# Sliding-window attention and a Silu expert layer on one core: attention per head pair in full-array matmuls, row loads cast on chip, an order laid by hand

## Chip, cores and metric

The kernel runs on one core of one Trainium2 chip. The metric is the device time of one execution in microseconds, the median over several runs. Engines are named as the profile names them: PE is TensorE's matmuls, PEld its weight loads, DVE is VectorE, ACT is ScalarE, POOL is GpSimd, SP is SyncE (here it only issues DMAs).

## What is computed

```python
# q, k, v: (8, 8, 576, 64) fp32: batch, head, position, width
scores = (1 / sqrt(64)) * (q @ k.transpose(0, 1, 3, 2))
rel = pos[:, None] - pos[None, :]
scores = where((rel >= 0) & (rel < 64), scores, -1e9)     # a causal window of 64
attn = exp(scores - scores.max(-1)); attn /= attn.sum(-1) + 1e-9
x = (attn @ v).transpose(0, 2, 1, 3).reshape(4608, 512)   # tokens x (heads, width)
h = x @ w_in                                              # 512 -> 2048
out = (h / (1 + exp(-h))) @ w_out                         # 2048 -> 512, fp32
```

## The kernel before

The sequence of 576 positions is cut into nine blocks of 64 queries. Since the window is 64, a block of queries needs 128 keys, its own 64 and the 64 before. Attention works on a pair of heads at a time (`emit_pair_attention`, line 179), 32 pairs in all.

- Loads. For each pair POOL issues two loads of q and two of k (line 187), which are cast from fp32 to bf16 on the way, and six loads of v (lines 199 to 207). v is loaded twice, once in chunks of 128 positions from 0 (`v_even`) and once shifted by 64 (`v_odd`), so that any window of 128 keys starts at partition 0. A 65th column of ones in each head gives the sum of the exponents. All weights are loaded and cast by the same POOL queue: w_in behind the third pair's loads (line 307), w_out behind the seventh's (line 309).
- Transposes. Six matmuls each bring q and k to width-major form (line 222); DVE copies q out of PSUM (line 231), ACT copies k (line 233).
- For each of the two heads: nine score matmuls that use one half of the array's rows (line 244), one exponent over 576 columns on ACT (line 253), one product with a 0/1 mask on DVE (line 255), nine value matmuls of 65 columns (line 263), one reciprocal and one product by it on DVE (lines 273 and 274).
- Nine transposes (line 281) and one copy on DVE (line 289) write the pair's outputs into `bridge`, the bf16 input of the expert layer, four tiles of 128 features by 4608 tokens.

The expert layer works on nine tiles of 512 tokens. The first GEMM of a tile is 16 x 4 matmuls of 512 columns, two output blocks at a time (`emit_moe1_pair`, line 124), each block followed by a Silu on ACT (line 139). The second is 4 x 16 matmuls (line 160), each 16 followed by a DVE copy out of PSUM (line 168) and a store that SP issues (line 170). The first GEMM of a tile is emitted when all pairs of the batches that it covers are emitted (line 314); second GEMMs wait in a list, one block of 128 tokens per pair (line 310). The first eight pairs are those of batches 0 and 1, in turns (line 295). The framework's scheduler orders each engine's instructions from this, by readiness and priority.

PSUM has three buffers for attention, transposes and second GEMMs together (`attn_ps`, line 79) and two for the first GEMM (line 82).

Of the kernel before, what the change touches and what calls it, by code (L numbers as in the profile page):

```python
# [9 lines left out]

MOE_ACT = mybir.ActivationFunctionType.Silu

MOE_UNITS_PER_PAIR = 5


def _build_block_mask(nc, mask, first):
    nc.gpsimd.memset(mask, 1.0)
    nc.gpsimd.affine_select(
        out=mask, in_=mask, compare_op=mybir.AluOpType.is_ge, fill=0.0,  # L20
        base=-1, channel_multiplier=1, pattern=[[-1, 64]],
    )
    nc.gpsimd.affine_select(
        out=mask, in_=mask, compare_op=mybir.AluOpType.is_ge, fill=0.0,
        base=64, channel_multiplier=-1, pattern=[[1, 64]],
    )
    if first:
        nc.gpsimd.affine_select(
            out=mask, in_=mask, compare_op=mybir.AluOpType.is_ge, fill=0.0,
            base=-64, channel_multiplier=1, pattern=[[0, 64]],  # L30
        )
# [3 lines left out]
def kernel(
    ctx: ExitStack,
    tc: tile.TileContext,
    q: bass.AP,
    k: bass.AP,
    v: bass.AP,  # L40
    moe_w_in: bass.AP,
    moe_w_out: bass.AP,
    out: bass.AP,
):
# [3 lines left out]
    d_model, d_ff = moe_w_in.shape
    n_tokens = B * S
    W = 64  # L50
    NBLK = S // W
    NCH = (S + 127) // 128
# [1 line left out]
    NFT = d_ff // 128
    NDC = d_model // 128
    TT = 512
    NTT = n_tokens // TT

    assert S == 576 and D == 64 and d_model == 512 and d_ff == 2048

    PVW = 65
    PVO = 57

    def pv_off(t):
        return PVO + PVW * t

    const_pool = ctx.enter_context(tc.tile_pool(name="const", bufs=1))
    wpool = ctx.enter_context(tc.tile_pool(name="wpool", bufs=1))
    bridge_pool = ctx.enter_context(tc.tile_pool(name="bridge", bufs=1))
    qk_pool = ctx.enter_context(tc.tile_pool(name="qk", bufs=4))  # L70
    qt_pool = ctx.enter_context(tc.tile_pool(name="qt", bufs=2))
    v_pool = ctx.enter_context(tc.tile_pool(name="v", bufs=4))
    e_pool = ctx.enter_context(tc.tile_pool(name="e", bufs=4))
    os_pool = ctx.enter_context(tc.tile_pool(name="os", bufs=4))
    rc_pool = ctx.enter_context(tc.tile_pool(name="rc", bufs=3))
    g_pool = ctx.enter_context(tc.tile_pool(name="g", bufs=18))
# [2 lines left out]
    attn_ps = ctx.enter_context(tc.tile_pool(name="attn_ps", bufs=3, space=bass.MemoryType.PSUM))
    tr_ps = attn_ps  # L80
    moe2_ps = attn_ps
    moe1_ps = ctx.enter_context(tc.tile_pool(name="moe1_ps", bufs=2, space=bass.MemoryType.PSUM))

    identb = const_pool.tile([128, 128], BF16)
    mask_blk = const_pool.tile([128, W], BF16)
    mask_head = const_pool.tile([128, S], BF16)

    def emit_consts():
        nc.gpsimd.memset(identb, 0.0)
# [261 lines left out]
```

## Time and profile before

| what | value |
|---|---|
| median of three runs | 424.79 us (424.58 to 426.48) |
| span of the profiled execution, first to last instruction | 422.7 us |
| PE busy | 351.0 us |
| POOL busy | 251.9 us |
| ACT busy | 174.6 us |
| DVE busy | 139.0 us |
| DMA packets | 157155, 32.49 MB |

The page gives the profiled execution's span, not a time of its own; the times of the runs are some 2 us longer than the span. Busy time of PE counts each matmul to its modelled end, so matmuls that follow each other closely overlap in it, and the distance between two starts is what one of them costs in a row of them. An "idle before" column says how long an engine stood before an instruction, and what ended that.

### The profile page before, as it was taken

To read this page: it belongs to the slowest core of one execution; us is meant where nothing else is said; L and a number is where in the kernel's file an instruction comes from. 1 tells how busy PE (TensorE), PEld (TensorE's weight loads), DVE (VectorE), ACT (ScalarE), POOL (GpSimd) and SP (SyncE) were. 2 spreads that over 40 slices of the span, in tenths; PEclk is the share of its full clock that TensorE was granted. 3 is DMA by queue.
4 is the path that set the end of the run, shared out by engine and by line. 5 is a ranking of instruction groups with operands and counts; after the bars stand their busy time and mean duration, and the time that the engine had idled before them with its cause. 6 is when DMAs were issued, how large, how long until landed. Compare 5 with 4: busy or idle time off the path is not lost.

```text
span 422.7 us, 7509 instructions
## 1 busy us (share of the span) xinstructions
PE 351.0 (83%) x2929; PEld 183.9 (44%) x2976; DVE 139.0 (33%) x292; ACT 174.6 (41%) x270; POOL 251.9 (60%) x493
## 2 busy tenths in 40 slices
PE   0452564799899989998999889988998999999996
PEld 0340453344444544454444544454444444444442
DVE  0350363032631463146314631463135215201011
ACT  1310223394256525651565166516552452342420
POOL 8995998999999798279827892789240000000000
PEclk9999999999999999999999999999999999999999
DMA  8999999999999999599958995899641011001011
GB/s 54 61 103 183 76 86 130 147 87 100 109 102 107 88 88 100 54 79 87 100 56 78 87 99 58 74 87 102 59 53 51 6 46 50 26 0 51 26 51 74
DMA packets 157155, 32.49 MB, mean 77 GB/s; under 512 B 149440, under 2 KB 151488, under 8 KB 157120
## 3 DMA queue, kind: packets, MB, share of 16 engines
q0 software_dynamic: 151936, 22.57, 75.1%
q1 hardware_dynamic: 5184, 9.44, 6.0%
q8 instruction: 24, 0.39, 0.4%
q14 instruction: 11, 0.09, 0.1%
HBM read 45.09 MB, written 9.44 MB: 129 GB/s over the span
## 4 chain that ended last, share of the span: by engine, by line
PE 57%; ACT 15%; POOL 11%; issue 8%; DMA 6%; DVE 2%; another core or an unknown queue 1%; ACTq 0%; POOLq 0%
PE ps L160 22%; PE psa L130 12%; PE psb L130 11%; PE sc_ps L263 5%; ACT e_t L253 5%; ACT gt L139 4%; ACT kt L233 3%; DMA q_nat<-in_q_dram 3%; ACT L253 3%; PE pst L222 3%; POOL q_nat L187 2%; POOL v_odd L207 2%; POOL k_nat L187 2%; PE sc_ps L281 2%; PE sc_ps L244 2%
## 5 line engine op out<-in xcount | busy, mean ns | idle before, releaser
L160 PE MATMUL ps<-w_out_sb,gt 128*128 128x512 bf16 x548 | 142.6, 381 | 2.2 <-issue 1.1
L130 PE MATMUL psa<-bridge,w_in_sb 128*128 128x512 bf16 x276 | 93.2, 383 | 7.8 <-ACT gt L139 4.2
L130 PE MATMUL psb<-bridge,w_in_sb 128*128 128x512 bf16 x281 | 94.0, 382 | 2.3 <-DMA w_in_sb<-in_moe_w_in_dram 1.8
L130 PEld LDWEIGHTS <-w_in_sb 128*128 128x128 bf16 x576 | 55.9, 98 | 76.0 <-issue 17.9
L139 ACT ACTIVATE gt<-psa 128x512 bf16<-128x512 f32 x72 | 43.0, 597 | 89.4 <-PE psa L130 76.0
L160 PEld LDWEIGHTS <-gt 128*128 128x128 bf16 x576 | 51.4, 98 | 54.8 <-ACT gt L139 0.3
L233 ACT COPY kt<-pst 128x576 bf16<-128x576 bf16 x32 | 20.5, 640 | 127.7 <-PE pst L222 123.2
L255 DVE TENSOR_TENSOR e_t<-e_t,mask_head 128x576 bf16<-128x576 bf16 x64 | 29.3, 458 | 109.7 <-ACT e_t L253 107.1
L187 POOL DMA_DIRECT2D q_nat<-in_q_dram x64 | 50.6, 846 | 21.9 <-PE pst L222 18.8
L207 POOL DMA_DIRECT2D v_odd<-in_v_dram x64 | 56.7, 885 | 0.8 <-DMA w_in_sb<-in_moe_w_in_dram 0.8
L199 POOL DMA_DIRECT2D v_even<-in_v_dram x64 | 55.2, 863 | 1.6 <-DMA q_nat<-in_q_dram 0.7
L168 DVE COPY ot<-ps 128x512 f32<-128x512 f32 x36 | 24.9, 691 | 94.1 <-PE ps L160 94.1
L187 POOL DMA_DIRECT2D k_nat<-in_k_dram x64 | 50.6, 841 | 4.5 <-PE pst L222 2.6
L274 DVE TENSOR_TENSOR o_sb<-sc_ps,rcol 64x576 bf16<-64x576 f32 x64 | 47.8, 747 | 1.9
L253 ACT ACTIVATE e_t<-sc_ps 128x576 bf16<-128x576 f32 x64 | 38.2, 648 | 13.7 <-PE sc_ps L244 13.5
L139 ACT ACTIVATE gt<-psb 128x512 bf16<-128x512 f32 x72 | 42.6, 592 | 0.0
L203 POOL DMA_DIRECT2D v_odd<-in_v_dram x64 | 41.7, 651 | 0.4 <-DMA w_in_sb<-in_moe_w_in_dram 0.4
L263 PE MATMUL sc_ps<-v_odd,e_t 128*64 128x65 bf16 x320 | 32.5, 210 | 8.7 <-ACT e_t L253 6.5
L263 PEld LDWEIGHTS <-e_t 128*64 128x64 bf16 x576 | 25.8, 120 | 27.4 <-DVE e_t L255 21.2
L222 PE MATMUL pst<-identb,q_nat 96*128 96x96 bf16 x192 | 16.9, 221 | 22.7 <-DMA q_nat<-in_q_dram 13.2
L244 PE MATMUL sc_ps<-qt,kt 64*128 64x64 bf16 x576 | 21.2, 200 | 16.0 <-ACT kt L233 15.1
L244 PEld LDWEIGHTS <-kt 64*128 64x128 bf16 x576 | 17.7, 100 | 25.5 <-issue 19.3
(32 smaller groups left out, 228.9 us busy)
## 6 DMA issues: line engine op xcount, KB each, us to landing
out_dram<-ot SPq DMA_DIRECT2D x36, 256.0 KB, 2.1
q_nat<-in_q_dram POOLq DMA_DIRECT2D x64, 72.0 KB, 3.1
k_nat<-in_k_dram POOLq DMA_DIRECT2D x64, 72.0 KB, 3.2
v_even<-in_v_dram POOLq DMA_DIRECT2D x64, 64.0 KB, 3.3
v_odd<-in_v_dram POOLq DMA_DIRECT2D x64, 64.0 KB, 3.0
w_in_sb<-in_moe_w_in_dram POOLq DMA_DIRECT2D x8, 256.0 KB, 8.3
w_out_sb<-in_moe_w_out_dram POOLq DMA_DIRECT2D x16, 128.0 KB, 5.0
v_odd<-in_v_dram POOLq DMA_DIRECT2D x64, 8.0 KB, 2.7
```

Source lines behind the costliest of these rows:

```text
L130: nc.tensor.matmul(ps1, lhsT=w_in_sb[:, c, ft * 128:(ft + 1) * 128], rhs=bridge[c][:, t0:t0 + TT], start=(c == 0), stop=(c == NDC - 1),)
L139: nc.scalar.activation(out=gt, in_=ps1, func=MOE_ACT)
L160: nc.tensor.matmul(ps2, lhsT=g_tiles[(j, fc)][:, idx * 128:(idx + 1) * 128], rhs=w_out_sb[:, fc, :], start=(fc == 0), stop=(fc == NFT - 1),)
L187: nc.gpsimd.dma_start(out=nat[:, :, c0:c0 + 64], in_=src[b, h0 + hh, :, :].rearrange("(c p) d -> p c d", p=96),)
L199: nc.gpsimd.dma_start(out=v_even[:, :, c0:c0 + 64], in_=v[b, h0 + hh, 0:512, :].rearrange("(c p) d -> p c d", p=128),)
L203: nc.gpsimd.dma_start(out=v_odd[64:128, 0, c0:c0 + 64], in_=v[b, h0 + hh, 0:64, :],)
L207: nc.gpsimd.dma_start(out=v_odd[:, 1:5, c0:c0 + 64], in_=v[b, h0 + hh, 64:576, :].rearrange("(c p) d -> p c d", p=128),)
L233: nc.scalar.copy(out=dst[:, off:off + S], in_=pst)
L244: nc.tensor.matmul(sc_ps[:, t * W:(t + 1) * W], lhsT=kt[base:base + 64, t * W: t * W + 128], rhs=qt[base:base + 64, t * W:(t + 1) * W], st ...
L253: nc.scalar.activation(out=e_t, in_=sc_ps[:, 0:S], func=mybir.ActivationFunctionType.Exp, scale=scale)
L263: nc.tensor.matmul(sc_ps[0:64, o0:o0 + PVW], lhsT=e_t[:, t * W:(t + 1) * W], rhs=vt[:, chv, hi * 65:(hi + 1) * 65], start=(t == 0 or t == ...
L274: nc.vector.tensor_mul(o_sb[:, :, base:base + 64], pv[:, :, 0:64], rcol[:, :, None].to_broadcast([64, NBLK, W]),)
```

## The change

The kernel is written anew around the same mathematics.

- q and k of a pair are loaded by one DMA each, as fp32 in rows of 512 bytes; SP issues them (POOL for pairs 4 to 7). They are cast to bf16 on chip: in the first batch by DVE (q) and ACT (k), later by POOL.
- v is loaded once, in three DMAs with a cast, and DVE copies it between the two halves of the partitions (`fix_v`).
- The transposed q of a pair is written into a tile `qbd` that holds head 0 in partitions 0 to 63 and head 1 in 64 to 127, each beside zeros. One matmul with all 128 rows of k then gives the scores of both heads for one block of queries, 128 columns; one value matmul with 128 exponent columns gives both heads' outputs, 130 columns, of which each head uses its half.
- A unit of attention is a group: a pair and three blocks of queries (`scores`, `values`, `to_bridge`). There are 96. The outputs are written into one of four zeroed tiles `obd`, and a matmul against two stacked unit matrices adds and transposes them; ACT copies the result to `bridge`.
- The order of the program is kept (`manual_schedule`). Batch 0 is prepared alone. A tile's first GEMM is emitted with the transposes of the next four pairs between its matmuls, one step after every six; its second GEMM with attention steps, one after every three. A step holds the scores of one group, the values of the group two steps back and the bridge matmuls of the group four steps back. Beside the nine second GEMMs stand 12, 8, 12, 12, 8, 12, 12, 8 and 0 groups.
- Tile 0's first GEMM is split into columns 0 to 192 and 192 to 512, and its second GEMM goes over all four token blocks at once, in order of the weights' arrival.
- PSUM is four buffers for both GEMMs and four for attention, used in turn.

```diff
+    ctx.enter_context(tc.manual_schedule())
...
+    moe_ps = ctx.enter_context(tc.tile_pool(name="moe_ps", bufs=4, space=bass.MemoryType.PSUM))
+    at_ps = ctx.enter_context(tc.tile_pool(name="at_ps", bufs=4, space=bass.MemoryType.PSUM))
...
+    def load_qk(u, eng):
+        b, pj = divmod(u, NP)
+        for nm, src in (("q", q), ("k", k)):
+            t = nat_pool.tile([96, 6, 128], FP32, name=f"{nm}_nat", tag=f"{nm}_nat")
+            eng.dma_start(
+                out=t,
+                in_=src[b, 2 * pj:2 * pj + 2].rearrange("h (g p c) d -> p (h g) (c d)", g=3, c=2),
+            )
+            nat[(nm, u)] = t
...
+    def load_w_in():
+        for f in range(8):
+            f0 = f * 256
+            nc.gpsimd.dma_start(
+                out=w_in_sb[:, :, f0:f0 + 256],
+                in_=w_in[:, f0:f0 + 256].rearrange("(c p) f -> p c f", p=128),
+            )
...
+    def cast(u, nm, copy):
+        t = natb_pool.tile([96, 6, 128], BF16, name=f"{nm}_natb", tag=f"{nm}_natb")
+        copy(
+            out=t.rearrange("p m (h d) -> p h m d", h=2),
+            in_=nat.pop((nm, u)).rearrange("p (h g) (c d) -> p h (g c) d", h=2, c=2),
+        )
...
+    def fix_v(u):
+        t = vv[u % NK].rearrange("p t (h x) -> p t h x", h=2)
+        nc.vector.tensor_copy(out=t[0:64, 2:9:2, :, 0:64], in_=t[64:128, 1:9:2, :, 0:64])
+        nc.vector.tensor_copy(out=t[64:128, 0:8:2, :, 0:64], in_=t[0:64, 1:9:2, :, 0:64])
...
+    def scores(u, g):
+        i = u % NK
+        sp = at_ps.tile([128, 3, 2, 64], FP32, name="sp", tag="ap")
+        for x in range(3):
+            t = 3 * g + x
+            nc.tensor.matmul(
+                sp[:, x], lhsT=kt[i][:, t * 64:t * 64 + 128],
+                rhs=qbd[i][:, :, t * 64:(t + 1) * 64],
+                start=(x == 0), stop=(x == 2),
+            )
+        e = e_pool.tile([128, 3, 2, 64], BF16, name="e", tag="e")
+        nc.scalar.activation(out=e, in_=sp, func=ACTF.Exp, scale=scale)
+        nc.vector.tensor_mul(e, e, mask0 if g == 0 else mask)
...
+    def values(u, g):
...
+        pv = at_ps.tile([128, 3, VW], FP32, name="pv", tag="ap")
+        for x in range(3):
+            nc.tensor.matmul(
+                pv[:, x, :], lhsT=e[:, x].rearrange("p h i -> p (h i)"),
+                rhs=vv[i][:, 3 * g + x, :], start=(x == 0), stop=(x == 2),
+            )
...
+        nc.vector.reciprocal(out=rc, in_=pv.rearrange("p x (h y) -> p x h y", h=2)[:, :, :, 64])
+        for hh in range(2):
+            p0 = hh * 64
+            nc.vector.tensor_mul(
+                ob[p0:p0 + 64, :, p0:p0 + 64],
+                pv[p0:p0 + 64, :, hh * 65:hh * 65 + 64],
+                rc[p0:p0 + 64, :, hh:hh + 1].to_broadcast([64, 3, 64]),
+            )
...
+    def to_bridge(u, g):
...
+        op = at_ps.tile([128, 3, 64], FP32, name="op", tag="ap")
+        for x in range(3):
+            nc.tensor.matmul(op[:, x, :], lhsT=ob[:, x, :], rhs=twoi,
+                             start=(x == 0), stop=(x == 2))
...
+        nc.scalar.copy(out=bridge[pj][:, c0:c0 + 192], in_=op.rearrange("p x i -> p (x i)"))
...
+    for u in range(4, 8):
+        load_qk(u, nc.gpsimd)
+    for f in range(4):
+        load_w_out(f)
+    for u in range(4, 8):
+        load_v(u)
+    for f in range(4, 8):
+        load_w_out(f)
...
+    interleave(mm1(0, 0, 192), 7, first, lead=2)
+    for i in range(4, 8):
+        zeros(i)
+    for u in range(4, 8):
+        cast(u, "q", pcopy)
+        cast(u, "k", pcopy)
...
+    for j in range(NTT):
...
+        for u in nxt:
+            load_qk(u, nc.sync)
+        interleave(mm1(j, 192, TT) if j == 0 else mm1(j), 6, ins, lead=30 if j == 0 else 4)
+        interleave(mm2(j, j == 0), 3, attention_steps(part[j]), lead=2)
+        for u in nxt:
+            load_v(u)
+            cast(u, "q", pcopy)
+            cast(u, "k", pcopy)
```

## Rows read from the trace of the kernel before

**Rows 1.** The page, part 1: busy us (share of the span) and instructions of each engine.
```profile
PE 351.0 (83%) x2929; PEld 183.9 (44%) x2976; DVE 139.0 (33%) x292; ACT 174.6 (41%) x270; POOL 251.9 (60%) x493
```

**Rows 2.** Stretches: length, then PE, PEld, DVE, ACT, POOL busy (instructions), clock, DMA.
```profile
0.00:75.00 75.00, 32.55 (x409) 24.39 (x413) 24.98 (x56) 16.46 (x25) 67.17 (x143) 1.00 1.14 101
...
214.79:257.43 42.64, 39.02 (x350) 20.36 (x356) 16.98 (x37) 21.02 (x33) 29.58 (x56) 1.00 0.92 80
361.90:418.70 56.80, 56.01 (x254) 24.55 (x254) 5.99 (x9) 17.36 (x32) 0.00 (x0) 1.00 0.10 38
418.70:422.70 4.00, 0.02 (x1) 0.00 (x0) 0.69 (x1) 0.00 (x0) 0.00 (x0) 1.00 0.17 66
```

**Rows 3.** Timeline of POOL, first 70 us: start, length, what [idle before <-releaser].
```profile
1.38 1.60 POOL L187 DMA_DIRECT2D q_nat<-in_q_dram  x2 [0.86 <-POOLq L335]
...
26.30 4.39 POOL L111 DMA_DIRECT2D w_in_sb<-in_moe_w_in_dram  x8
...
39.92 0.76 POOL L207 DMA_DIRECT2D v_odd<-in_v_dram  x1 [0.78 <-DMA w_in_sb<-in_moe_w_in_dram]
...
43.47 1.49 POOL L187 DMA_DIRECT2D q_nat<-in_q_dram  x2
...
47.33 0.58 POOL L203 DMA_DIRECT2D v_odd<-in_v_dram  x1
...
50.72 1.55 POOL L187 DMA_DIRECT2D q_nat<-in_q_dram  x2
```

**Rows 4.** Timeline of PE, at 73 us and in the period from 214.79.
```profile
73.18 1.44 PE L130 MATMUL psa<-bridge,w_in_sb 128*128 128x512 bf16 x3 [0.69 <-ACT gt L139]
...
219.49 2.76 PE L160 MATMUL ps<-w_out_sb,gt 128*128 128x512 bf16 x12
222.44 0.22 PE L263 MATMUL sc_ps<-v_odd,e_t 128*64 128x65 bf16 x1 [0.19 <-ACT e_t L253]
...
222.72 0.20 PE L263 MATMUL sc_ps<-v_odd,e_t 128*64 128x65 bf16 x1
222.85 0.39 PE L160 MATMUL ps<-w_out_sb,gt 128*128 128x512 bf16 x1
...
225.84 0.43 PE L281 MATMUL sc_ps<-identb,o_sb 64*128 64x64 bf16 x9
...
226.25 0.42 PE L222 MATMUL pst<-identb,k_nat 96*128 96x96 bf16 x6
```

**Rows 5.** Groups by line and shape, whole run: busy us, mean ns | idle before.
```profile
L274 DVE TENSOR_TENSOR o_sb<-sc_ps,rcol 64x576 bf16<-64x576 f32 x64 | 47.8, 747 | 1.9
L139 ACT ACTIVATE gt<-psa 128x512 bf16<-128x512 f32 x72 | 43.0, 597 | 89.4 <-PE psa L130 76.0 <-PE ps L160 7.0 <-remote 6.3
...
L253 ACT ACTIVATE e_t<-sc_ps 128x576 bf16<-128x576 f32 x64 | 38.2, 648 | 13.7 <-PE sc_ps L244 13.5
...
L255 DVE TENSOR_TENSOR e_t<-e_t,mask_head 128x576 bf16<-128x576 bf16 x64 | 29.3, 458 | 109.7 <-ACT e_t L253 107.1
...
L168 DVE COPY ot<-ps 128x512 f32<-128x512 f32 x36 | 24.9, 691 | 94.1 <-PE ps L160 94.1
...
L253 ACT ACT_TABLE_LOAD x14 | 18.0, 1283 | 0.2
...
L273 DVE RECIPROCAL rcol<-sc_ps 64x9 f32<-64x9 f32 x64 | 13.2, 207 | 5.6 <-PE sc_ps L263 5.1
...
L97 POOL COPY mask_head<-mask_blk 128x64 bf16<-128x64 bf16 x8 | 1.5, 280 | 0.0
...
L89 POOL MEMSET identb<- 128x128 bf16 x1 | 0.3, 302 | 0.0
L18 POOL MEMSET mask_head<- 128x64 bf16 x1 | 0.2, 248 | 0.0
```

**Rows 6.** Timeline of ACT and DVE in the period from 214.79: exponents, mask products.
```profile
221.25 1.19 ACT L253 ACTIVATE e_t<-sc_ps 128x576 bf16<-128x576 f32 x2
221.93 1.00 DVE L255 TENSOR_TENSOR e_t<-e_t,mask_head 128x576 bf16<-128x576 bf16 x2 [6.90 <-ACT e_t L253]
```

More of the change, by code (lines that the diff above doesn't have):

```diff
@@ L10 @@
 BF16 = mybir.dt.bfloat16
[L12 to L31, printed above, removed]
@@ L34, with kernel @@
-@with_exitstack
[L35 to L44, printed above, removed]
+ACTF = mybir.ActivationFunctionType
+GE = mybir.AluOpType.is_ge
+@with_exitstack
+def kernel(ctx, tc, q, k, v, w_in, w_out, out):
     nc = tc.nc
     B, H, S, D = q.shape
[L48 to L52, printed above, removed]
-    scale = 1.0 / float(D) ** 0.5
[L54 to L76, printed above, removed]
-    o_pool = ctx.enter_context(tc.tile_pool(name="o", bufs=4))
[L79 to L89, printed above, removed]
@@ new lines, in transposes @@
+    def transposes(u, nm, copies):
+        t = natb.pop((nm, u))
+        pst = at_ps.tile([128, 6, 96], BF16, name="pst", tag="ap")
+        for m in range(6):
+            nc.tensor.matmul(
+                pst[:, m, :], lhsT=t[:, m, :], rhs=ident[0:96, 0:96],
+                is_transpose=True, start=(m == 0), stop=(m == 5),
+            )
+        src = pst.rearrange("x (g c) p -> x g p c", c=2)
+        if nm == "q":
+            d = qbd[u % NK].rearrange("x h (g p c) -> x h g p c", g=3, c=2)
+            copies[0](out=d[0:64, 0], in_=src[0:64])
+            copies[1](out=d[64:128, 1], in_=src[64:128])
+        else:
+            d = kt[u % NK][:, 64:64 + S].rearrange("x (g p c) -> x g p c", g=3, c=2)
+            copies[0](out=d, in_=src)
@@ new lines, in interleave @@
+    def interleave(stream, every, steps, lead=0):
+        steps = iter(steps)
+        for n, _ in enumerate(stream):
+            if n >= lead and (n - lead) % every == 0:
+                st = next(steps, None)
+                if st is not None:
+                    st()
+        for st in steps:
+            st()
+    vcopy, acopy, pcopy = nc.vector.tensor_copy, nc.scalar.copy, nc.gpsimd.tensor_copy
+    groups = {b: [(4 * b + pj, g) for g in range(NG) for pj in range(NP)] for b in range(B)}
@@ new lines @@
+    todo = [gr for b in range(1, B) for gr in groups[b]]
+    beside = [12, 8, 12, 12, 8, 12, 12, 8, 0]
+    part, last = [], []
+    for n in beside:
+        part.append(todo[:n])
+        todo = todo[n:]
+        last.append(max([u for u, _ in part[-1]] + last[-1:]))
+    for u in range(4):
+        load_qk(u, nc.sync)
+    consts()
+    for u in range(4):
+        load_v(u)
+    load_w_in()
+    for i in range(4):
+        zeros(i)
+    nc.vector.tensor_copy(out=twoi[0:64, :], in_=ident[0:64, 0:64])
@@ new lines @@
+    nc.vector.tensor_copy(out=twoi[64:128, :], in_=ident[64:128, 64:128])
+    nc.vector.tensor_copy(out=mask0, in_=mask)
+    nc.vector.memset(mask0[0:64, 0], 0.0)
+    for i in range(NOB):
+        nc.vector.memset(obd[i].bitcast(FP32), 0.0)
+    first = list(attention_steps(groups[0], ahead=2))
+    for u in range(4):
+        cast(u, "q", vcopy)
+        cast(u, "k", acopy)
+        transposes(u, "q", (vcopy, acopy))
+        transposes(u, "k", (acopy,))
+        fix_v(u)
+        if u >= 2:
+            first.pop(0)()
```

342 lines of the change are left out of this document (143 added, 199 removed).

## The prediction, made before the changed kernel ran

> **What bounds the kernel now.** I read the page first, then the stretches by stage, then the queue of each engine inside a stretch. On the page TensorE is busy 351.0 of 422.7 us, GpSimd 251.9 and VectorE 139.0 [rows 1]. The stretches say which of them holds each stage. In the first 75 us GpSimd is busy for 67.17 and TensorE for 32.55; from 129.48 to 300.09 one period of 42.65 us, a batch each, comes four times, with 39.02 us of TensorE and 29.58 of GpSimd in it; and the last 57 us are nearly all expert matmuls [rows 2].
>
> What fills the first 75 us is GpSimd issuing loads. Its timeline starts one pair's loads at 43.47 and the next pair's at 50.72, so 7.25 us a pair whatever TensorE does: four loads of q and k at 0.75 each, v in six pieces, four memsets [rows 3]. Eight pairs are loaded before the first expert tile starts at about 72 us. The weights stand in the same queue: eight loads of w_in issued from 26.30 in 4.39 us, and a load behind them still waits for one of them at 39.92, 13.6 us later [rows 3].
>
> The period I price by the distance between starts, not by the busy column. Twelve matmuls of 512 columns cover 2.76 us with a last one of 0.38, so 0.216 each; six transposes of 96 columns 0.42 with a last of 0.21, so 0.042; nine of 64 columns 0.43, so 0.030; nine of 65 columns from 222.44 to 222.72, so 0.035 [rows 4]. A period is then 128 x 0.216 + 48 x 0.042 + 108 x 0.030 + 72 x 0.035 = 35.4 us, and 7.2 us are waits. That is about what can be gained in each of them; the start holds the rest. At 73.18 three matmuls of 512 columns take 1.44 us, where 0.216 apart they would take 0.81 [rows 4]: that is the lower of TensorE's two clock levels (1.2 and 2.4 GHz), though the clock column of the stretches reads 1.00 there [rows 2]. TensorE had been mostly idle before it.
>
> **The change part by part.** *Full-array attention matmuls.* A pair had 18 score and 18 value matmuls of 64 and 65 columns; it gets 9 and 9 of 128 and 130. The columns that stream through are the same, so at 0.418 ns a column (from 0.042 at 96 and 0.216 at 512) they cost 0.056 each, 1.0 us a pair as against 1.2. By itself this part is worth nearly nothing; the trace has none of 128 columns; the bounds are 0.042 and 0.216, nearest to the lower one. What changes is the evacuation: three groups a pair, each with one exponent, one mask product, one reciprocal and two products.
>
> *The start.* One batch, not two, is prepared, q and k of it on SP's queue. GpSimd's queue up to the second expert GEMM of tile 0 decides, I think. Launch and constants about 3.2 us (the first load now goes at 1.38 [rows 3], and some six constants at about 0.3 [rows 5]); 12 loads of v, per pair two as dear as a load of q and one of the short kind at 0.58 [rows 3], 8.3; 8 of w_in, in more and shorter rows, at 0.75 like q's rows (bounds 0.55, today's, and 0.75), 6. The loads of q and k for pairs 4 to 7 stand behind these and wait for w_in to land, as the load at 39.92 does now: first issue at 11.5 plus 13.6, so 25, and one more issue, 26. Then 4 of w_out at 0.55 (as w_in's now), 12 of v, 4 of w_out: 12.7, so 38.6. Then eight casts of 96x768 float to bf16, which TensorE's transposes for tile 0 wait for. The nearest rows are a 128x64 copy of 0.28 and memsets of 0.248 and 0.302 for 64 and 128 columns [rows 5]: by that slope, 0.84 ns a column, a cast is 0.87 and 0.8 in a stream; by the copy's 4.4 ns a column throughout it is 3.4. I take 0.8, since the slope comes from two rows; the start ends at 38.6 + 6.4 + 1 = 46. VectorE reaches the same point by about 38 (memsets 8, four pairs at 3, the steps of batch 0 at 8 to 16, by the rates below), so it is cover with 8 us to spare, and GpSimd's turn. Below, 40; above, 67.
>
> *After 46 us* TensorE has left: 64 + 8 x 128 expert matmuls at 0.216, 235.0; 84 groups of attention at 3 x (0.056 + 0.056 + 0.030) = 0.425, 35.8; transposes of 24 pairs, 288 x 0.042, 12.1. The 64 extra matmuls of the split tile 0 lie before 46.
>
> *The steps.* Fixed and per-element prices of VectorE and ScalarE come from pairs of rows: 64x576 in 0.747 and 128x512 in 0.691 on VectorE is 1.04 ns an element plus 0.15; the mask product of 576 in 0.458 goes at half that per element; ScalarE's 576 in 0.648 and 512 in 0.595 is 0.83 plus 0.17 [rows 5]. A group's exponent (384) is then 0.49, its mask product 0.36, its reciprocal 0.21 like today's [rows 5], its two products (192 each) 0.35 each. VectorE has 1.26 us in a step for which TensorE has 0.425 + 3 x 0.216 = 1.07. And the four PSUM buffers go round: a full step takes three, so the third matmul group of a step needs the buffer that the step before gave to its values, and that comes free when VectorE has done both products. From the first score matmul: last one ends at 0.33, exponent 0.37 to 0.86, mask to 1.25, reciprocal to 1.43, products to 2.1, seen at 2.16 (hand-overs of about 0.04: the first of the two exponents from 221.25 lasts 0.65, and the mask product starts at 221.93 [rows 5, 6]). The next step's third group then goes at 2.16, and after its 0.09 and three expert matmuls the step after begins: two steps in 2.90, so 1.45 each and a wait of 0.38. Full steps (all three parts present) are 8 of a 12-group part and 4 of an 8-group part: 5 x 8 + 3 x 4 = 52, so 19.8 us. Without the buffer wait it is 0; at one and a half times these VectorE durations two steps take 3.53, a wait of 0.69 each, 36.
>
> *Smaller terms.* The 0.69 us copy of each finished output tile [rows 5] stands in the same VectorE queue; in 13 cases it falls between full steps and moves the mask product by 0.5: 6.5. At each second GEMM the first exponent waits behind the last Silu and a table load of 1.28 [rows 5], about 0.85 beyond TensorE's cover: 8 x 0.85 = 6.8. Going from a short matmul to a 512 one starts 0.13 after the last, not 0.035 [rows 4]: 0.09 on the 44 steps that do not wait anyway, 4. At 46 VectorE is behind with the four pairs' copies (11.6 us of work from 39.5 on), which holds the first values up by 4, and TensorE, idle before, starts its dense work at the lower clock, as at 73.18 [rows 4], where the matmuls stood 0.43 apart; taken for some 4 us, 2: 6. The end is as now, 4.0 from the last matmul on [rows 2].
>
> What I cost at nothing, and its cover: v is shifted by VectorE instead of loaded twice; with the copies of q and k that is 2.9 us a pair (two copies of 576 at 0.75, two of 512 at 0.68), 11.6 a tile under a first GEMM of 15.9, and if that cover fails it is the excess per tile. The casts and 12 loads of v are 15 us of GpSimd a tile of 40. SP's loads of the next four pairs each wait for a cast to free a buffer, and the output stores are queued behind them; the casts are done a GEMM earlier. Silu, 16 x 0.6 [rows 5], and the q copies stay under the first GEMM.
>
> **Sum:** 46 + 235.0 + 35.8 + 12.1 + 19.8 + 6.5 + 6.8 + 4 + 6 + 4.0 = 376.0 us of span. The profiled execution's span is 422.7, the median 424.79, so 2.1 us lie outside: 378 us against 424.79.
>
> No row shows VectorE and GpSimd reading on-chip memory together; GpSimd's only copies now are eight at the start [rows 5]. The Trainium skill, "SBUF — State Buffer" (Who interferes with whom), says that a VectorE instruction with two inputs there and a GpSimd one that reads there lock each other out for a whole instruction. The mask product and the cast are such a pair; by this rule the sum would be about 390, the third rival.
>
> **The rivals.**
> - *No waits in the steps* (341): the buffers or VectorE are quicker than priced and the four smaller waits go too, less 37 of waits. For it: today's period loses only 7.2 us on a longer chain. Against it: 1.26 exceeds 1.07 anyhow.
> - *Dear casts* (400): 3.4 us each moves the start to 67. Per tile GpSimd would have 8 x 3.4 + 8.3 = 35.5 us, just under a tile, so no more than the start is lost. For it: 0.28 for 64 columns. Against it: the two memsets.
> - *Casts and mask products exclude each other* (390): 48 casts of 0.87 stand beside 84 mask products in tiles of 40 us; casts fill a sixth of the time, so 14 meetings at up to 0.87, 12 us. All of them meeting is 42 us, 420.
> - *VectorE becomes the bound* (430, slower): its place is every tile after 46 us. At my durations it has 197 us there (six first GEMMs at 11.6, five second ones at 12 x 1.26 + 4 x 0.69 = 17.9, three with 8 groups at 12.8); the stretches without it, start, last tile, end, add 94. It decides from 1.44 times my durations on (378 = 94 + 1.44 x 197) and makes the kernel slower from 1.7 times on: 94 + 1.7 x 197 = 430. For it: strided two-byte reads and shifts between partition halves have no row. Against it: today's product of 576 and copy of 512 fit one price [rows 5].
>
> **How the numbers follow.** The forecast gets 0.43, no waits 0.24, dear casts 0.13, exclusion 0.08, VectorE 0.12, of which 0.03 within 0.5% of now (2.1 us, about what a measurement of this kernel can tell from no change) and 0.09 above. Faster is 0.88. The range reaches from just under the no-wait case, 338, to just over the dear casts, 404; what is left out is VectorE's 0.12 and the lower third of the no-wait case.
>
> **What would show it.** In the changed profile: first matmul of tile 0's second GEMM near 46 us, with GpSimd full until the casts; full steps 1.4 to 1.5 us apart, the wait before the bridge matmuls ended by VectorE's products; VectorE near 240 us in all; GpSimd well under 200; a tile with twelve groups near 40 us, one with eight near 36. It is wrong if casts last over 2 us, if steps follow each other at 1.1 or at 2 us, or if TensorE waits on transposes in tiles 1 to 6.

## The result, and the profile of the kernel after

The changed kernel takes 396.21 us (median of 4 runs, 395.85 to 396.95) against 424.69: a ratio of 0.932, 95% interval 0.929 to 0.935, so 28.5 us less. The profiled execution's span is 394.6, and 1.6 us lie outside.

The page's part 1, as [rows 1]:

```profile
PE 329.4 (83%) x2423; PEld 180.0 (46%) x2464; DVE 232.9 (59%) x596; ACT 206.3 (52%) x410; POOL 133.4 (34%) x185
```

GpSimd falls from 251.9 to 133.4 us, VectorE rises from 139.0 to 232.9, TensorE loses 21.6. The stretches, cut by this kernel's stages: the start to the second GEMM of tile 0, that GEMM and a whole period from tile 2's second GEMM to tile 3's; columns as in [rows 2]:

```profile
0.00:61.20 61.20, 31.29 (x332) 25.71 (x333) 37.05 (x122) 30.44 (x70) 48.66 (x73) 0.97 1.25 192
61.20:89.25 28.05, 22.82 (x173) 12.40 (x174) 23.37 (x57) 13.85 (x31) 11.76 (x16) 0.94 0.56 54
141.87:183.70 41.83, 36.84 (x280) 19.50 (x284) 27.96 (x68) 23.60 (x46) 15.12 (x20) 1.00 0.55 97
```

The start is 61.2 us long, with TensorE busy for half of it. A period with twelve groups lasts 41.83 us, with 36.84 of TensorE: 5.0 are waits. GpSimd's queue in the start, as [rows 3], then VectorE's in the same time:

```profile
14.18 6.30 POOL L87 DMA_DIRECT2D w_in_sb<-in_moe_w_in_dram  x8 [0.91 <-DMA vv<-in_v_dram]
...
20.46 0.77 POOL L65 DMA_DIRECT2D q_nat<-in_q_dram  x1
...
30.68 0.73 POOL L65 DMA_DIRECT2D q_nat<-in_q_dram  x1 [3.01 <-DVE q_natb L126]
...
46.48 2.86 POOL L93 DMA_DIRECT2D w_out_sb<-in_moe_w_out_dram  x4
49.27 0.90 POOL L126 CAST q_natb<-q_nat 96x768 bf16<-96x768 f32 x1
...
54.66 0.86 POOL L126 CAST k_natb<-k_nat 96x768 bf16<-96x768 f32 x1
```
```profile
11.87 0.07 DVE L121 MEMSET vv<- 128x18 bf16 x1 [10.04 <-DMA vv<-in_v_dram]
...
19.68 0.49 DVE L126 CAST q_natb<-q_nat 96x768 bf16<-96x768 f32 x1
```

On GpSimd the loads of q and k stand from 20.46 to 32.13, one of them for 3.01 us because VectorE has not yet cast an earlier pair out of its buffer; w_out is issued until 49.3, and the eight casts last until 55.5. On VectorE a memset that writes the column of ones into v, between the columns that the loads fill, was emitted behind the loads of v into the same buffers, so it waits 10.04 us for one to land (the memset of a block of v that no load writes went at 1.72 without a wait). The first cast, which stands behind it, comes at 19.68; e1_zeros_first below, where the zeros stand ahead of the loads, has it at 7.13. TensorE's first instruction is at 20.22. Its first expert matmul, its first transpose behind GpSimd's casts, and the first of tile 0's second GEMM:

```profile
41.46 0.67 PE L226 MATMUL ps<-bridge,w_in_sb 128*128 128x192 bf16 x3
...
54.48 0.42 PE L136 MATMUL pst<-ident,q_natb 96*128 96x96 bf16 x6
...
61.20 0.38 PE L250 MATMUL ps<-w_out_sb,gt 128*128 128x512 bf16 x1
```

No wait stands before the transpose at 54.48: pair 4's cast of q is done at 50.17, and TensorE is still in expert matmuls until then. From 41.46 to 61.2 TensorE never stands for GpSimd; its waits lie before, the last of them 1.21 us for VectorE's products of batch 0.

In the kernel before, the stream of expert matmuls begins at 71.91 (four single ones stand ahead of it, between 31.96 and 57.46):

```profile
71.91 0.58 PE L130 MATMUL psa<-bridge,w_in_sb 128*128 128x512 bf16 x1 [0.55 <-DVE bridge L289]
```

From there on both kernels take about as long, 422.7 - 71.9 = 350.8 us before and 394.6 - 41.5 = 353.1 now. So the 28 us lie in the start. It is not the same work, though: 25 pairs of attention were left at that point before, 28 are left now, and the rest of the kernel takes three more pairs in for 2.3 us.

The groups of the new VectorE and GpSimd work, as [rows 5]: busy us, mean ns of one, idle before.

```profile
L187 DVE TENSOR_TENSOR obd<-pv,rc 64x192 bf16<-64x192 f32 x192 | 68.2, 355 | 4.6
L169 DVE TENSOR_TENSOR e<-e,mask 128x384 bf16<-128x384 bf16 x96 | 43.0, 452 | 49.5 <-ACT e L168 47.1
L126 POOL CAST k_natb<-k_nat 96x768 bf16<-96x768 f32 x28 | 25.4, 906 | 0.4 <-PE ps L226 0.3
L143 DVE COPY qbd<-pst 64x576 bf16<-64x576 bf16 x32 | 24.0, 749 | 11.1 <-PE pst L136 11.0
...
L152 DVE COPY vv<-vv 64x512 bf16<-64x512 bf16 x32 | 13.0, 408 | 0.4
```

A step as VectorE's timeline shows it, where no cast runs, and above it tile 0's steps while GpSimd casts; then GpSimd in that time:

```profile
61.41 1.17 DVE L151 COPY vv<-vv 64x512 bf16<-64x512 bf16 x1
62.59 1.48 DVE L152 COPY vv<-vv 64x512 bf16<-64x512 bf16 x1
64.11 0.75 DVE L143 COPY qbd<-pst 64x576 bf16<-64x576 bf16 x1
...
67.36 2.79 DVE L169 TENSOR_TENSOR e<-e,mask 128x384 bf16<-128x384 bf16 x3 [0.19 <-ACT e L168]
...
73.79 0.36 DVE L169 TENSOR_TENSOR e<-e,mask 128x384 bf16<-128x384 bf16 x1
74.18 0.20 DVE L184 RECIPROCAL rc<-pv 128x6 f32<-128x6 f32 x1
74.41 0.72 DVE L187 TENSOR_TENSOR obd<-pv,rc 64x192 bf16<-64x192 f32 x2
75.16 0.36 DVE L169 TENSOR_TENSOR e<-e,mask 128x384 bf16<-128x384 bf16 x1
```
```profile
61.56 0.85 POOL L126 CAST q_natb<-q_nat 96x768 bf16<-96x768 f32 x1
62.33 0.94 POOL L126 CAST k_natb<-k_nat 96x768 bf16<-96x768 f32 x1
63.21 1.53 POOL L75 DMA_DIRECT2D vv<-in_v_dram  x2
...
66.07 0.94 POOL L126 CAST k_natb<-k_nat 96x768 bf16<-96x768 f32 x1
66.97 1.53 POOL L75 DMA_DIRECT2D vv<-in_v_dram  x2
```

The quiet step is 75.16 - 73.79 = 1.37 us, and VectorE has no idle time in it: 0.36 + 0.20 + 0.72 and three gaps of 0.03. Beside the casts, and shortly after them, three mask products take 2.79 us together (0.36, 0.95 and 1.53), and the two copies of v 1.17 and 1.48, where the quietest ones take 0.29; the copy of q out of PSUM between them takes its 0.75 as everywhere. (GpSimd's spans are rough in the profile; that its load issues, which stand there too, are not the cause is seen below.)

### The profile page after: what moved, and what is told of

Read it like the earlier page. It is cut to its first block, busy times and chain, and to the rows that moved or that the text cites. A ratio compares the mean times of both kernels' runs of the same rounds, so it can differ in the third digit from the quotient of the medians.

```text
span 394.6 us, 6598 instructions
## 1 busy us (share of the span) xinstructions
PE 329.4 (83%) x2423; PEld 180.0 (46%) x2464; DVE 232.9 (59%) x596; ACT 206.3 (52%) x410; POOL 133.4 (34%) x185
## 4 chain that ended last, share of the span: by engine, by line
PE 51%; DVE 32%; ACT 6%; issue 5%; POOL 2%; DMA 2%; DVEq 0%; ACTq 0%; POOLq 0%
PE ps L226 28%; PE ps L250 15%; DVE obd L187 13%; DVE e L169 7%; DVE rc L184 4%; PE pst L136 4%; ACT L168 2%; DVE ot L238 2%; PE pv L177 2%; DMA vv<-in_v_dram 2%; ACT e L168 2%; DVE qbd L143 2%; ACT gt L233 1%; POOL vv L75 1%; DVE vv L151 1%
## 5 line engine op out<-in xcount | busy, mean ns | idle before, releaser
L226 PE MATMUL ps<-bridge,w_in_sb 128*128 128x512 bf16 (+2 forms) x624 | 135.2, 359 | 0.9
L233 ACT ACTIVATE gt<-ps 128x512 bf16<-128x512 f32 (+2 forms) x160 | 84.6, 555 | 46.8 <-PE ps L226 45.3
L75 POOL DMA_DIRECT2D vv<-in_v_dram x64 | 49.1, 773 | 131.4 <-PE pv L177 90.6
L169 DVE TENSOR_TENSOR e<-e,mask 128x384 bf16<-128x384 bf16 x96 | 43.0, 452 | 49.5 <-ACT e L168 47.1
L187 DVE TENSOR_TENSOR obd<-pv,rc 64x192 bf16<-64x192 f32 x192 | 68.2, 355 | 4.6
L168 ACT ACTIVATE e<-sp 128x384 bf16<-128x384 f32 x96 | 44.7, 491 | 33.9 <-PE sp L162 33.8
L202 ACT CAST bridge<-op 128x192 bf16<-128x192 f32 x96 | 30.6, 318 | 45.6 <-PE op L199 44.3
L177 PE MATMUL pv<-vv,e 128*128 128x130 bf16 x288 | 33.8, 228 | 11.9 <-DVE e L169 6.8
L162 PEld LDWEIGHTS <-kt 128*128 128x128 bf16 x288 | 25.2, 104 | 24.0 <-issue 2.9
L162 PE MATMUL sp<-qbd,kt 128*128 128x128 bf16 x288 | 33.2, 231 | 3.1 <-ACT kt L147 1.4
L177 PEld LDWEIGHTS <-e 128*128 128x128 bf16 x288 | 21.9, 101 | 20.9 <-DVE e L169 10.8
L199 PEld LDWEIGHTS <-obd 128*128 128x128 bf16 x288 | 15.7, 99 | 33.2 <-DVE obd L187 32.8
L126 POOL CAST q_natb<-q_nat 96x768 bf16<-96x768 f32 x28 | 24.7, 881 | 13.3 <-DMA q_nat<-in_q_dram 13.3
```

What stands on the lines that cost most here:

```text
L75: nc.gpsimd.dma_start(out=t[:, 1:9:2, hh * 65:hh * 65 + 64], in_=v[b, 2 * pj + hh, 0:512, :].rearrange("(c p) d -> p c d", p=128),)
L162: nc.tensor.matmul(sp[:, x], lhsT=kt[i][:, t * 64:t * 64 + 128], rhs=qbd[i][:, :, t * 64:(t + 1) * 64], start=(x == 0), stop=(x == 2),)
L168: nc.scalar.activation(out=e, in_=sp, func=ACTF.Exp, scale=scale)
L169: nc.vector.tensor_mul(e, e, mask0 if g == 0 else mask)
L177: nc.tensor.matmul(pv[:, x, :], lhsT=e[:, x].rearrange("p h i -> p (h i)"), rhs=vv[i][:, 3 * g + x, :], start=(x == 0), stop=(x == 2),)
L187: nc.vector.tensor_mul(ob[p0:p0 + 64, :, p0:p0 + 64], pv[p0:p0 + 64, :, hh * 65:hh * 65 + 64], rc[p0:p0 + 64, :, hh:hh + 1].to_broadcast([ ...
```

## The experiments

Three questions: what sets the start, what sets a step, and whether casts lengthen VectorE's work. All lengths of a second GEMM below run from its first matmul to the next first GEMM's, read from TensorE's timeline; "12" are tiles 2, 3, 5 and 6, "8" tiles 1, 4 and 7.

| kernel | tile 0: second GEMM begins, lasts | "12" | "8" | time, us |
|---|---|---|---|---|
| after the change | 61.2, 28.1 | 26.0, 26.0, 25.4, 24.0 | 20.8, 21.9, 20.4 | 396.21 |
| e1_zeros_first | 60.2, 26.9 | 26.0, 26.0, 25.4, 24.0 | 20.5, 21.9, 20.4 | 393.92 |
| e2_zeros_casts | 55.2, 30.6 | 26.0, 26.0, 25.4, 24.0 | 20.9, 22.0, 20.4 | 391.77 |
| e3_at5 | 63.0, 27.2 | 26.0, 26.0, 25.0, 24.0 | 20.5, 22.0, 20.4 | 397.43 |
| e4_ot_act | 61.1, 26.7 | 24.7, 24.7, 24.0, 22.8 | 20.5, 21.4, 19.8 | 389.29 |
| e5_every | 61.5, 23.7 | 23.2, 23.2, 23.2, 21.5 | 17.3, 18.8, 17.4 | 374.3 |
| e6_more_casts | 64.3, 28.7 | 28.9 in all | 24.1, 23.8, 23.8 | 428.88 |
| e7_casts_late | 63.7, 24.5 | 24.0 in all | 20.4 in all | 388.24 |
| e8_mask_pool | 62.0, 21.8 | 20.9 in all | 18.9 in all | 367.27 |
| e9_all | 59.8, 21.3 | 20.0 in all | 17.8 in all | 362.54 |
| e10_all_sp | 58.1, 21.3 | 20.0 in all | 17.8 in all | 360.51 |
| e11_order | 54.5, 20.7 | 20.0 in all | 18.2, 17.8, 17.8 | 350.46 |

**The start.** e1_zeros_first writes the zeros and ones before the loads:

```diff
     consts()
-    for u in range(4):
-        load_v(u)
-    load_w_in()
     for i in range(4):
         zeros(i)
...
     for i in range(NOB):
         nc.vector.memset(obd[i].bitcast(FP32), 0.0)
+    for u in range(4):
+        load_v(u)
+    load_w_in()
```

> Only the order of the start changes: VectorE's memsets for pairs 0 to 3, masks and zero tiles are emitted ahead of the loads of v, so the memset of v's columns of ones no longer waits for v to land. If VectorE's queue set the start (its first cast of q at 19.7 us), the cast goes at 7 to 8 us, tile 0's second GEMM starts 10 to 12 us earlier than 61.2 and the time falls from 396 to about 385. If GpSimd's queue sets it, as the prediction had it, the first GEMM starts near 31 us instead of 41.5, but the eight casts still stand behind GpSimd's loads: the second GEMM starts near 57.5 and the time falls by 3 to 4 us, to about 392.

Ratio 0.927 (0.923 to 0.932), which overlaps the interval of the change itself. The first GEMM of tile 0 begins at 31.6 instead of 41.5, 9.9 us sooner, and the second only 1.0 sooner, nearer to what was expected if GpSimd's queue sets the start. What has come in between stands in TensorE's timeline:

```profile
51.66 0.66 PE L136 MATMUL pst<-ident,q_natb 96*128 96x96 bf16 x6 [6.90 <-POOL q_natb L126]
```

GpSimd's first cast begins at 50.70 there. So two chains of nearly equal length end at about 60: VectorE's, late by its memset, and GpSimd's queue, loads and casts. In the changed kernel VectorE's is the longer one; taking it away shows the other. e2_zeros_casts takes the casts of pairs 4 to 7 off GpSimd as well, and writes the zeros of all eight buffer sets first:

```diff
-    for i in range(4):
+    for i in range(8):
         zeros(i)
...
-    for i in range(4, 8):
-        zeros(i)
     for u in range(4, 8):
-        cast(u, "q", pcopy)
-        cast(u, "k", pcopy)
+        cast(u, "q", vcopy)
+        cast(u, "k", acopy)
```

> As the run before, with the memsets of pairs 4 to 7 also at the front, and the casts of pairs 4 to 7 on VectorE (q) and ScalarE (k) instead of GpSimd. If VectorE's queue alone set the start, this gives no more than the run before (about 385). If GpSimd's queue is the second limit, the transposes of pairs 4 to 7 no longer wait for it: tile 0's second GEMM starts near 48 to 50 us and the time is about 384, some 8 us under the run before.

Ratio 0.920 (0.916 to 0.924); the second GEMM begins at 55.2, 6.0 us sooner. The 48 to 50 and the 384 us that were expected did not come: the first GEMM begins at 33.2, and from there TensorE goes through its matmuls and transposes until 55.2 with one wait of 1.49 us, so here its own work sets the end of the start. The second GEMM takes 2.6 us longer: TensorE stands 1.41 us for a Silu where it stood 0.31, and 3.46 instead of 1.87 for a mask product. Beside GpSimd's casts for tile 1 two copies of v last 1.82 and 1.93, and three mask products 3.11 from 62.35 on (2.79 in the changed kernel).

**A step.** The prediction put a wait for the PSUM buffers into each full step. e3_at5 gives attention a fifth buffer, from the expert GEMMs' four (tile 0's second GEMM then runs row block by row block as the others do):

```diff
-    moe_ps = ctx.enter_context(tc.tile_pool(name="moe_ps", bufs=4, space=bass.MemoryType.PSUM))
-    at_ps = ctx.enter_context(tc.tile_pool(name="at_ps", bufs=4, space=bass.MemoryType.PSUM))
+    moe_ps = ctx.enter_context(tc.tile_pool(name="moe_ps", bufs=3, space=bass.MemoryType.PSUM))
+    at_ps = ctx.enter_context(tc.tile_pool(name="at_ps", bufs=5, space=bass.MemoryType.PSUM))
...
-        interleave(mm2(j, j == 0), 3, attention_steps(part[j]), lead=2)
+        interleave(mm2(j, False), 3, attention_steps(part[j]), lead=2)
```

> Five PSUM buffers for attention and three for the GEMMs (tile 0's second GEMM block by block, since its four blocks at once need four buffers). Steps stand 1.37 us apart now. If they wait for the buffer that VectorE's two products give back, as the prediction had it, a fifth buffer takes that wait away: steps near 1.28 or less, 52 full steps, 5 us or more off, 391. If VectorE itself is full (0.36 + 0.20 + 0.72 and three hand-overs of 0.03 make 1.37), steps stay at 1.37 and the time stays within 1.5 us of 396.

Ratio 0.936 (0.932 to 0.940); from tile 1 on every second GEMM is within 0.4 us of its length in the changed kernel, and the quiet steps still follow each other at 1.37:

```profile
315.42 0.36 DVE L169 TENSOR_TENSOR e<-e,mask 128x384 bf16<-128x384 bf16 x1
...
316.79 0.36 DVE L169 TENSOR_TENSOR e<-e,mask 128x384 bf16<-128x384 bf16 x1
```

So the buffer does not set the pace; VectorE is simply full, as the quiet step above shows. e4_ot_act takes 0.69 us per output copy off VectorE:

```diff
-nc.vector.tensor_copy(out=ot, in_=ps)
+nc.scalar.copy(out=ot, in_=ps)
```

> The copy of a finished output block out of PSUM moves from VectorE (0.69 us) to ScalarE; nothing else changes. If VectorE's queue sets the length of the second GEMMs, about 17 of the 32 copies stand in its full stretch and the time falls by 17 x 0.72 = 12 us, to about 384, the second GEMMs with 12 groups from 25.9 to about 24. If the steps wait on buffers and TensorE, it is the prediction's 6.5 us at most, 390. If ScalarE's queue is as full as VectorE's, nothing is gained.

Ratio 0.915 (0.912 to 0.918), 6.9 us less, which is nearer to the 6.5 of the buffers than to the 12 of a full VectorE, so the time by itself does not tell the two apart. The 12 counted 17 copies among the steps. In a tile with twelve groups only two of the four stand there: the mask products around them are 2.1 and 1.26 us apart in the changed kernel and 1.37 and 1.38 here, 0.6 us a copy, and such a tile is 1.2 to 1.4 us shorter. e5_every leaves all work where it is and only gives VectorE's step more of TensorE's work beside it:

```diff
-interleave(mm2(j, j == 0), 3, attention_steps(part[j]), lead=2)
+interleave(mm2(j, j == 0), 4 if len(part[j]) > 8 else 5, attention_steps(part[j]), lead=2)
```

> Attention steps of a second GEMM are laid after every 4th matmul (12 groups) or 5th (8 groups) instead of every 3rd; nothing else. Theory A (VectorE's 1.28 us of work per step, 1.37 with the gaps, sets the pace, and the matmuls left over when the steps are done come behind it): TensorE now has 4x0.216+0.44 = 1.30 us of its own per step, so little of its time is spent waiting and no tail of matmuls is left; 12-group second GEMMs go from 25.9 to about 22 to 23.5 us, 8-group ones from 20.8 to about 18.5 to 19, about 20 us in all: 372 to 380 us. Rival B (the length comes from what stands at the two ends of a tile, the table load, the first three exponentials, the last ot copies, and not from the steps): lengths unchanged within 0.5 us, 394 to 398 us.

Ratio 0.878 (0.875 to 0.882), 21.9 us less, every second GEMM beside steps 2.2 to 4.3 us shorter. In the changed kernel the steps run out with 16 of the GEMM's 64 matmuls left, 3.5 us with nothing beside them (the row counts 15; by the distance of 0.31 us before it the trace lacks the first):

```profile
164.27 0.26 PE L199 MATMUL op<-twoi,obd 128*128 128x64 bf16 x3
164.58 3.40 PE L250 MATMUL ps<-w_out_sb,gt 128*128 128x512 bf16 x15
167.82 1.24 PE L226 MATMUL ps<-bridge,w_in_sb 128*128 128x512 bf16 x5
```

VectorE's pace and this tail add up; spread, the 16 matmuls go into the waits. e8_mask_pool takes the mask product of batches 1 to 7 off VectorE:

```diff
-nc.vector.tensor_mul(e, e, mask0 if g == 0 else mask)
+(nc.vector if u < 4 else nc.gpsimd).tensor_mul(e, e, mask0 if g == 0 else mask)
```

> From the second batch on the mask product goes to GpSimd (84 of 96 groups); VectorE's step is left with reciprocal and two products, 0.92 us, 0.98 with gaps. Theory A (VectorE paces the steps): if GpSimd's product takes less than 1.0 us, steps go from 1.37 to TensorE's own 1.09 us apart, 12-group second GEMMs from 25.9 to about 22.5, 8-group from 20.8 to about 18.7, 370 to 380 us. Rival B (GpSimd's product takes 1.4 us or more, or its loads and casts stand ahead of the products in its queue): steps 1.4 us apart or more, ended by GpSimd, 395 to 415 us. Rival C (the steps don't set the length): 394 to 398 us with VectorE's busy time down by about 38 us.

Ratio 0.862 (0.859 to 0.865), 28.9 us less, more than A's 370 to 380 allowed for. GpSimd's product takes 0.91 us, two and a half times VectorE's 0.36, and the steps are nevertheless 1.07 to 1.08 us apart, TensorE's own time:

```profile
L169 POOL TENSOR_TENSOR e<-e,mask 128x384 bf16<-128x384 bf16 x84 | 75.9, 910 | 104.4 <-ACT e L168 102.5
...
286.74 0.81 PE L250 MATMUL ps<-w_out_sb,gt 128*128 128x512 bf16 x3
287.39 0.33 PE L162 MATMUL sp<-qbd,kt 128*128 128x128 bf16 x3
...
288.46 0.33 PE L162 MATMUL sp<-qbd,kt 128*128 128x128 bf16 x3
...
289.54 0.33 PE L162 MATMUL sp<-qbd,kt 128*128 128x128 bf16 x3
```

Part of this gain is not VectorE's pace: with the mask product off VectorE it no longer meets GpSimd's casts, and that alone takes tiles 2 and 3 from 26.0 to 24.0 (e7_casts_late below). The rest of the way, from 24.0 to 20.9, is VectorE's pace.

**Casts against mask products.** e6_more_casts adds two casts per step that nothing needs:

```diff
         ets[(u, g)] = e
+        if u >= 4:
+            nc.gpsimd.tensor_copy(out=probe, in_=e[:, 0, 0, 0:2])
+            for _ in range(2):
+                nc.gpsimd.tensor_copy(out=idle_b, in_=idle_f)
```

> GpSimd gets two casts more per step from tile 0's second GEMM on, 96x768 fp32 to bf16 out of a buffer of zeros that nothing else uses, ordered behind the step's mask product by a two-column copy (84 steps x 1.7 us = 143 us more of GpSimd's time; outputs unchanged). Theory A (a cast on GpSimd and a VectorE operation that reads and writes SBUF alone exclude each other; those with a PSUM operand go on): the mask product's mean rises from 0.45 to 0.8 us or more, the products out of PSUM stay at 0.355 and the reciprocal at 0.194, and VectorE's step grows from 1.37 to 1.8 us or more: 12-group second GEMMs 25.9 to 29 or more, 8-group 20.8 to 23 or more, 415 to 430 us in all. Rival B (no exclusion; the long mask products have another cause): the mask product stays at 0.45 and the second GEMMs within 0.5 us, 394 to 400 us, what changes being only that GpSimd's loads and casts come some us later.

The time is 428.88, 32.7 us more than the changed kernel's (ratio to the kernel before 1.007, 1.004 to 1.010). Its VectorE groups, and three steps of its timeline:

```profile
L173 DVE TENSOR_TENSOR e<-e,mask 128x384 bf16<-128x384 bf16 x96 | 68.2, 713 | 39.6 <-ACT e L172 37.2
L195 DVE TENSOR_TENSOR obd<-pv,rc 64x192 bf16<-64x192 f32 x192 | 68.2, 355 | 4.6
```
```profile
199.22 0.99 DVE L173 TENSOR_TENSOR e<-e,mask 128x384 bf16<-128x384 bf16 x1
...
201.11 0.89 DVE L173 TENSOR_TENSOR e<-e,mask 128x384 bf16<-128x384 bf16 x1
...
203.02 0.77 DVE L173 TENSOR_TENSOR e<-e,mask 128x384 bf16<-128x384 bf16 x1
```

The mask product goes from 452 to 713 ns, in these steps to 0.77 to 0.99, and a step to 1.9 us; the products out of PSUM stay at 355 to the nanosecond. e7_casts_late is the opposite: the casts of a tile wait for its last mask product.

```diff
         for u in nxt:
             load_v(u)
+        if nxt and last_e[0] is not None:
+            nc.gpsimd.tensor_copy(out=probe, in_=last_e[0][:, 0, 0, 0:2])
+        for u in nxt:
             cast(u, "q", pcopy)
             cast(u, "k", pcopy)
```

> GpSimd's casts of each tile are held back, by a two-column copy out of the tile's last masked e, until VectorE has finished the tile's mask products. Theory A (exclusion): the mask product's mean falls from 0.45 to 0.36 to 0.38, fix_v's two copies in tile 0 come back to 0.29 each, VectorE's busy time falls by 8 to 14 us; tile 0's second GEMM shortens by 2 to 4 us, the others by up to 1, and the time falls by 4 to 9 us, less what the late casts cost the transposes at the start of the next first GEMM (none if these still start at once): 387 to 393 us. Rival B (no exclusion): the mean stays at 0.45, and the time stays or grows by the late casts, 395 to 402 us.

Ratio 0.912 (0.909 to 0.915), 8.0 us less than the changed kernel, with the same work. The mask product's group:

```profile
L171 DVE TENSOR_TENSOR e<-e,mask 128x384 bf16<-128x384 bf16 x96 | 34.1, 358 | 51.3 <-ACT e L170 48.7
```

Its mean is 358 ns, although GpSimd goes on issuing v's loads beside these steps: the casts are what lengthens it. (A copy of v can be longer beside load issues alone, where no cast has run yet: 0.50 us at 24.53 in the changed kernel, 25 us before GpSimd's first cast.) All four tiles with twelve groups now take 24.0 us, as tile 6 did before, beside whose steps there are no casts; the gain is 5.3 us there, 1.8 in the tiles with eight and 3.5 in tile 0, less a start that came 2.5 later (already TensorE's first transposes, which the edit doesn't touch, came 1.4 later).

**Put together.** e9_all joins e1's order, e2's casts, e8 and e5:

> The zeros ahead of the loads, the casts of pairs 4 to 7 on VectorE and ScalarE, the mask products of batches 1 to 7 on GpSimd and the steps after every 4th (8 groups: 5th) matmul, together. Theory A (VectorE paces the steps and, with GpSimd's queue, the start): the first GEMM of tile 0 begins at about 31.5, its second at 52 to 54 (61.5 in the kernel after the change), 12-group second GEMMs take 19.2 to 20.3 us (25.9), 8-group ones 17.3 to 17.8 (20.8): 345 to 356 us. Rival B (the parts give the same gain twice: with the product off VectorE, spreading the steps brings nothing more): 12-group second GEMMs stay at 20.9, 355 to 362 us.

Ratio 0.852 (0.850 to 0.855). The steps did what A said, 20.0 and 17.8 us. The start did not: tile 0's second GEMM begins at 59.8 instead of 52 to 54, and 362.54 lies above A's 356 and just above B's 362. In this order the zeros of pairs 4 to 7 are again emitted behind the loads of their v; VectorE's timeline shows the same wait as in the changed kernel, now ahead of the casts that have moved to VectorE, and TensorE's shows what it costs:

```profile
45.51 0.07 DVE L121 MEMSET vv<- 128x18 bf16 x1 [4.90 <-DMA vv<-in_v_dram]
```
```profile
50.94 0.66 PE L136 MATMUL pst<-ident,q_natb 96*128 96x96 bf16 x6 [4.18 <-DVE q_natb L126]
51.40 1.80 PE L226 MATMUL ps<-bridge,w_in_sb 128*128 128x320 bf16 x6
...
56.74 0.98 PE L226 MATMUL ps<-bridge,w_in_sb 128*128 128x320 bf16 x6
```

e10_all_sp, `load_qk(u, nc.gpsimd)` to `load_qk(u, nc.sync)` for pairs 4 to 7:

> The kernel of e9_all, with the loads of q and k of pairs 4 to 7 issued by SyncE's queue instead of GpSimd's. GpSimd no longer stands in them from 20 to 31 us, so w_out and v of pairs 4 to 7 are issued some 10 us sooner. Theory A (GpSimd's queue still sets the beginning of tile 0's second GEMM): it begins 3 to 8 us sooner than in e9_all, and the time falls by as much. Rival B (after the first two parts TensorE's own matmuls at the lower clock and the transposes set it, or the DMA engines, which are busy all through): it begins within 1.5 us of e9_all's, and the time is the same within 2 us.

Ratio 0.848 (0.846 to 0.850), 1.7 us sooner (58.1) and 2.0 less: nearer to B, but not for B's reason, since TensorE still stands 3.94 us for the casts. e11_order changes the order alone, in three places at once:

```diff
     for i in range(4):
         zeros(i)
+    for i in range(8):
+        zeros_v(i)
...
             transposes(u, "k", (vcopy,))
-            fix_v(u)
...
+        for u in new:
+            fix_v(u)
         interleave(mm2(j, j == 0), ...
         for u in nxt:
-            load_v(u)
             cast(u, "q", pcopy)
             cast(u, "k", pcopy)
+        for u in nxt:
+            load_v(u)
```

> The kernel of e10_all_sp in another order: the zeros and ones of all eight v buffers are written before any v load (those of q and k of pairs 4 to 7 stay where they are); the copies of v from one half to the other are issued after a tile's first GEMM instead of inside it; and in each tile GpSimd casts q and k before it loads v. Theory A (what e9_all and e10_all_sp lost is VectorE's queue standing still at a memset or copy that waits for a v load, with casts and copies of q and k behind it): TensorE's wait of 3.9 us for the casts in tile 0 goes and the second GEMM of tile 0 begins at 53 to 55 instead of 57.7; the first GEMMs, 16.5 to 18.4 us in tiles 1, 3, 4, 5 and 6, return to 15.9; 348 to 353 us. Rival B (the casts and v loads come too late on GpSimd whatever the order, its mask products standing ahead of them): the first GEMMs stay long or the second GEMMs begin with a wait for v; 356 to 361 us.

Ratio 0.823 (0.821 to 0.826). The second GEMM of tile 0 begins at 54.5, the first GEMMs of tiles 1 to 6, 16.5 to 18.4 us in five of them in e10_all_sp, are all 15.9, and 350.46 us beats both kernels: 46 us under the changed one. Which of the three changes gave how much was not taken apart. Of its start of 54.5 us TensorE is busy for 32.0, and 22.3 are tile 0's first GEMM; what would shorten it further was not tried.

## Why the prediction was right, and where it was not

The forecast of 378 was 18 us too low; the range and the sign held. That the range held is in part luck: its upper end, 404, stood for dear casts, which did not come. What did come is a longer start, 15.2, and casts that lock out mask products, 10.6, less 7.2 by which the tiles had been priced too dear.

*The start, 46: this step failed, and it is 15.2 of the 18 us.* It let GpSimd's queue decide and took VectorE as cover ("VectorE reaches the same point by about 38 ... so it is cover"). In the changed kernel VectorE decides: its queue stands behind a memset that waits for a load, which I had counted by its work and not by what it waits for, so its products of batch 0 end at 49.1, the first expert matmul comes at 41.46, and from there TensorE's own matmuls and transposes, with no wait on GpSimd, run until 61.2. GpSimd's queue is nearly as long, and it failed in three of its terms. v ended at 14.2 instead of 11.5, with waits for earlier pieces to land that I had not counted. The loads of q and k ended at 32.1 instead of 26: the last one that waits for w_in goes at 26.2, 12.0 after the first of w_in (13.6 was taken), but from there it is four issues and not one, and a wait of 3.0 for VectorE's cast stands among them. And w_out, v, w_out took 17.2 (32.1 to 49.3) instead of 12.7. The casts were right, 0.77 apart and 6.2 in all, so the rival of dear casts fell; as the price came from two memsets, that was partly luck. The single us between the casts and the second GEMM was 5.7: the eight sets of transposes are laid between matmuls, 1.07 us apart, and run from 54.5 to 61.2. e1 shows that neither chain alone was the start.

*Matmuls and transposes* held: first GEMMs of 15.88 us against 64 x 0.216 + 48 x 0.042 = 15.84, three score matmuls in 0.17, TensorE without a wait on transposes in tiles 1 to 6.

*The steps, 1.45 by the buffers.* The size was nearly right, 1.37, and the mechanism wrong. The prices held: mask product 0.36, reciprocal 0.20, two products 0.72. With gaps that is 1.37 of VectorE alone; I had added them to 1.26, seen that this exceeds TensorE's 1.07, and still let the buffer set the pace. The row without idle time on VectorE and e3 (a fifth buffer, steps still at 1.37) speak against the buffer. e4, e5 and e8, which relieve VectorE or give it time, all gain, as VectorE's work explains; they would gain in a wait for its products too, so they do not decide it. The sign that was named, waits before the bridge matmuls ended by VectorE's products, is there (13.7 us of them after 61.2), and fits both accounts.

*Casts and mask products exclude each other*, given 0.08 at 12 us more, is what happens, and costs 10.6 us in the second GEMMs, 8.0 in all (e7, whose start came later). The Trainium skill, "SBUF — State Buffer" (Who interferes with whom), says so for an operation with two inputs there, and also for copies in the modes that use both ports, which the prediction had not drawn on. e6 and e7 agree for the mask product, 713 and 358 ns. The copies of v, up to 1.93 instead of 0.29 beside casts, fit the second half of the rule; whether they run in such a mode, no trace shows.

*What balanced.* From tile 0's second GEMM on, 333.4 us of the span were left instead of 330.0 (376.0 - 46). With the 5.3 + 1.8 + 3.5 = 10.6 of the exclusion taken off, the tiles were priced 7.2 too dear. Which of the waits and small terms hold the 7.2 was not measured one by one. Shifting v by VectorE was priced at 0.68 a copy and takes 0.29 where no cast runs.

*VectorE becomes the bound*, the slower rival: it does become the bound of the second GEMMs, but at my durations, not at 1.44 times them, and that is not slower. e6 shows how far it is: with mask products of 713 ns the kernel is level with the one before.

## What to carry to other kernels

Ask of the first instruction in a queue what it waits for, not only how long it works: a memset of 0.07 us emitted behind a load into the same stretch of a tile held VectorE's queue up for 10 us here, and for 4.9 in e9, where TensorE stood 4.2 for it. Then ask which queue is next: with VectorE's wait gone, GpSimd's queue let the start shrink by only 1.0 us. When steps are laid by hand into a stream of matmuls, compare the busiest engine's work per step with TensorE's, and spread the steps over the whole stream, so that no tail of matmuls is left behind them: 22 us for one number. Before giving the second engine more SBUF work, look whether the first one's operands lie in SBUF beside it; the engine that is slower for an operation (0.91 against 0.36) may still be the right place for it.
